# A transformer block with adaptive layer norm: three small moves around the K, Q and first MLP stages

## The chip, the cores and the metric

The kernel runs on one core of one Trainium2 chip. The metric is device time in microseconds (us); lower is better. The median of three runs of the kernel before is 244.02 us (243.87 to 244.14). One profiled execution of it took 243.82 us; its trace spans 242.1 us from the first to the last instruction, and all moments below are us from the start of that span.

## The reference

One block of a diffusion transformer: two batches of 256 tokens, width D = 1152, two heads of 576, MLP width F = 4608. A conditioning vector `c` gives six modulation vectors; the ones that matter here are `shift_a` and `scale_a` (first layer norm) and `shift_m` and `scale_m` (second).

```python
mod = (_silu(c) @ w_mod).reshape(B, 6, 1, D)
shift_a, scale_a, gate_a, shift_m, scale_m, gate_m = [mod[:, i] for i in range(6)]
h = _layernorm(x, axis=-1) * (1 + scale_a) + shift_a
qkv = (h @ wqkv).reshape(B, N, 3, H, Dh)
q, k, v = (qkv[:, :, 0].copy(), qkv[:, :, 1].copy(), qkv[:, :, 2].copy())
attn = _softmax(jnp.einsum('bqhd,bkhd->bhqk', q, k) * Dh ** (-0.5), axis=-1)
a = jnp.einsum('bhqk,bkhd->bqhd', attn, v).reshape(B, N, D) @ wo
x = x + gate_a * a
h2 = _layernorm(x, axis=-1) * (1 + scale_m) + shift_m
m = _gelu(h2 @ w_fc1) @ w_fc2
return x + gate_m * m
```

A shift added to all keys of a batch moves every score of one query by the same amount, which the softmax cancels. So the kernel computes K from `hT0` (normalized and scaled, not yet shifted) and adds `shift_a` only afterwards, for Q and V.

## The kernel before

P is 128, KD = D/P = 9 chunks of the width, T = 512 tokens. Activations are held transposed: chunk k is a tile of 128 features by 512 tokens, 256 of each batch b.

**Loads for K.** `w_k` has nine rows of 128 inputs. Columns 0 to 767 of each row come in a load of their own; the last 384 columns of all nine rows come in one load behind them, and then the shift weights. All loads of this part go through one queue (SyncE's).

```python
KGROUPS = [(0, 2), (2, 4), (4, 6), (6, 9)]
KM1 = 6
for g, (k0, k1) in enumerate(KGROUPS):
    load_scale_group(g, nc.sync)
    for k in range(k0, k1):
        nc.sync.dma_start(w_k[:, k, 0:KM1 * P], wqkv_v[:, k, D:D + KM1 * P])
nc.sync.dma_start(w_k[:, :, KM1 * P:D], wqkv_v[:, :, D + KM1 * P:2 * D])
...
w_shift_a = load_section("w_shift_a", S_SHIFT_A)     # three loads of three rows
w_q = wide_tile("w_q")
...
```

**End of K, the shift section, start of Q.** Output tiles 0 to 5 of K accumulate row by row as chunks arrive; tiles 6, 7 and 8 follow as whole panels of nine matmuls (L318 in the trace). The shift section is 36 narrow matmuls (L432) into `pn`, which VectorE transposes into `shift_a` (L438). VectorE (L454) and ScalarE (L456) then add the shift to each half chunk, and Q starts (L511). `k_evac(8)` copies K's last tile out of PSUM (L305 on VectorE); its accumulator is the one that Q's sixth matmul needs.

```python
k_panel(6)
k_evac(6)
k_panel(7)
k_evac(7)
k_panel(8, 0, 5)
shift_a = vec_section(sT, w_shift_a, "shift_a")
k_panel(8, 5)

hT = act.tile([P, KD, T], BF16, name="hT")
for k in range(KD):
    for b in range(B):
        dst, src = hT[:, k, b * N:(b + 1) * N], hT0[:, k, b * N:(b + 1) * N]
        if (k * B + b) % 3 < 2:
            nc.vector.tensor_scalar_add(dst, src, shift_a[:, k, b:b + 1])          # L454
        else:
            nc.scalar.activation(dst, src, ACT.Identity, bias=shift_a[:, k, b:b + 1])  # L456
    if k == 2:
        k_evac(8)
...
pq = [acc_tile([P, T], "pacc") for _ in range(KM1)]     # "acc" has 6 buffers
for k in range(KD):
    for m in range(KM1):
        nc.tensor.matmul(pq[m][:], w_q[:, k, m * P:(m + 1) * P], hT[:, k, :], ...)  # L511
```

**Second layer norm and the start of the MLP.** The output projection runs in groups (L705). Each is gated by VectorE (L710, reads PSUM), added to `x` by GpSimd (L711; VectorE for two of them) and measured by VectorE (L717). A normalized token tile t goes through a transposing DMA (L676) into `hT`; each chunk is then modulated in place: for batch 0 by ScalarE (L687) but for chunk 8, which is GpSimd's (L683); for batch 1 by ScalarE or VectorE (L691). The MLP's first matmul stage (FC1, L802) begins with batch 0 and takes chunks 0 to 8 in order.

```python
def ln2_modulate(b, ks=range(KD)):
    for k in ks:
        h = hT[:, k, b * N:(b + 1) * N]
        if b == 0 and k == KD - 1:
            nc.gpsimd.tensor_scalar(h, h, scale_m[:, k, b:b + 1], shift_m[:, k, b:b + 1], ...)   # L683
        elif b == 0 or k % 3 == 2:
            nc.scalar.activation(h, h, ACT.Identity, bias=shift_m[...], scale=scale_m[...])      # L687
        else:
            nc.vector.tensor_scalar(h, h, scale_m[...], shift_m[...], ...)                       # L691
...
wo_group(3, 0)
ln2_modulate(0, range(6))
ln2_stats(2, 2)
ln2_sqrt(2)
ln2_modulate(0, range(6, KD))
wo_group(3, 1)
ln2_stats(3, 0)
ln2_recip(2)
ln2_normalize(2)
ln2_transpose(2)
wo_group(3, 2)
wo_group(3, 3)
ln2_stats(3, 1)
ln2_stats(3, 2)
ln2_stats(3, 3)
ln2_sqrt(3)
ln2_recip(3)
ln2_normalize(3, 4 * P)
ln2_transpose(3)
...                                     # FC1, batch 0: 12 output tiles, then batch 1
```

[...]

Of the kernel before, what the change touches and what calls it, by code (L numbers as in the profile page):

```python
# [19 lines left out]
def kernel(  # L20
# [11 lines left out]
    nc = tc.nc  # L32
    B, N, D = x.shape
# [3 lines left out]
    P = 128  # L37
# [3 lines left out]
    KD = D // P  # L41
# [17 lines left out]
    def acc_tile(shape, name, dt=FP32):  # L59
        return psum.tile(shape, dt, name=name, tag="acc", bufs=6)  # L60
# [8 lines left out]
    wqkv_v = wqkv.rearrange("(k p) n -> p k n", p=P)  # L69
# [7 lines left out]
    def wide_tile(name):  # L77
        return wide.tile([P, KD, D], BF16, name=name, tag="wide")
# [19 lines left out]

    KGROUPS = [(0, 2), (2, 4), (4, 6), (6, 9)]
    KM1 = 6  # L100
    w_scale_a = wide_tile("w_scale_a")
    w_k = wide_tile("w_k")

    def load_scale_group(g, eng):
        c0, c1 = KGROUPS[g][0] * P, KGROUPS[g][1] * P
        eng.dma_start(w_scale_a[:, :, c0:c1], wmod_v[:, :, S_SCALE_A * D + c0:S_SCALE_A * D + c1])

    for g, (k0, k1) in enumerate(KGROUPS):
        load_scale_group(g, nc.sync)
        for k in range(k0, k1):  # L110
            nc.sync.dma_start(w_k[:, k, 0:KM1 * P], wqkv_v[:, k, D:D + KM1 * P])
    nc.sync.dma_start(w_k[:, :, KM1 * P:D], wqkv_v[:, :, D + KM1 * P:2 * D])

    def load_section(name, s, w=None):
        w = wide_tile(name) if w is None else w
# [12 lines left out]
    for r in range(0, KD, 3):  # L128
        nc.sync.dma_start(w_q[:, r:r + 3, 0:KM1 * P], wqkv_v[:, r:r + 3, 0:KM1 * P])
    nc.sync.dma_start(w_q[:, :, KM1 * P:D], wqkv_v[:, :, KM1 * P:D])  # L130
    w_scale_m = wide_tile("w_scale_m")
# [96 lines left out]
    def norm1(t, c0, c1, eng):  # L228
        if eng == "a":
            nc.scalar.activation(  # L230
                xns[t][:, c0:c1], x_sb[:, t, c0:c1], ACT.Identity,
                bias=nb1[:, t:t + 1], scale=rstd1[:, t:t + 1],
            )
        else:
            nc.vector.tensor_scalar(
                xns[t][:, c0:c1], x_sb[:, t, c0:c1], mv1[:, t, 0:1], rstd1[:, t:t + 1],
                op0=ALU.subtract, op1=ALU.mult,
            )
# [30 lines left out]
    def modulate(pt, i, k, t0, j0, w, eng):  # L269
        b = t0 // TPB  # L270
        dst, src, sc = hT0[:, k, t0 * P:t0 * P + w], pt[:, i, j0:j0 + w], scale_a[:, k, b:b + 1]
        if eng == "d":
            nc.vector.tensor_scalar_mul(dst, src, sc)
        else:
            nc.scalar.mul(dst, src, sc)
# [7 lines left out]

    def k_step(k, c0=0, c1=T, m0=0, m1=KM1):
        for m in range(m0, m1):
            if k == 0 and c0 == 0:
                pk[m] = acc_tile([P, T], "pk")
            nc.tensor.matmul(  # L288
                pk[m][:, c0:c1], w_k[:, k, m * P:(m + 1) * P], hT0[:, k, c0:c1],
                start=(k == 0 and c0 == 0), stop=(k == KD - 1), skip_group_check=True,  # L290
            )
# [19 lines left out]
    def k_evac(m):  # L311
        evac(kT[:, m, :], pk[m][:])

    def k_panel(m, ka=0, kb=KD):
        if ka == 0:
            pk[m] = acc_tile([P, T], "pk")
        for k in range(ka, kb):
            nc.tensor.matmul(  # L318
                pk[m][:], w_k[:, k, m * P:(m + 1) * P], hT0[:, k, :],
                start=(k == 0), stop=(k == KD - 1),  # L320
            )
# [70 lines left out]
    for k in range(2):  # L392
        modulate(pt_4, k, k, 3, 0, P, "d")
    k_step(3, 0, N, 3, KM1)
    norm1(1, CUT, D, "d")
# [31 lines left out]
    def vec_section(stat, w, name, nk=KD):  # L427
        pn = aux_tile([P, nk * 32], "pn")
        for k in range(KD):
            wk4 = w[:, k, :].rearrange("p (j q r) -> p q j r", q=4, r=32)  # L430
            for i in range(4):
                nc.tensor.matmul(  # L432
                    pn[32 * i:32 * i + SW, :].rearrange("p (j r) -> p j r", r=32),
                    stat[:, k, :], wk4[:, i, :, :],
                    start=(k == 0), stop=(k == KD - 1), tile_position=(0, 32 * i),
                )
        dst = act.tile([P, nk, 32], FP32, name=name)
        nc.vector.transpose(dst[:].rearrange("p k c -> p (k c)"), pn[:])  # L438
        return dst
# [2 lines left out]
    k_evac(6)  # L442
    k_panel(7)
    k_evac(7)
    k_panel(8, 0, 5)
    shift_a = vec_section(sT, w_shift_a, "shift_a")
    k_panel(8, 5)

    hT = act.tile([P, KD, T], BF16, name="hT")
    for k in range(KD):  # L450
        for b in range(B):
            dst, src = hT[:, k, b * N:(b + 1) * N], hT0[:, k, b * N:(b + 1) * N]
            if (k * B + b) % 3 < 2:
                nc.vector.tensor_scalar_add(dst, src, shift_a[:, k, b:b + 1])  # L454
            else:
                nc.scalar.activation(dst, src, ACT.Identity, bias=shift_a[:, k, b:b + 1])  # L456
        if k == 2:
            k_evac(8)
# [195 lines left out]
    def ln2_sqrt(t):  # L654
        nc.vector.bn_aggr(mv2[:, t, :], stats2[t][:, 0:nst[t], :].rearrange("p a b -> p (a b)"))
        rstds[t] = small.tile([P, 1], FP32, name="rstd", tag="rstd")
        nc.scalar.activation(rstds[t][:], mv2[:, t, 1:2], ACT.Sqrt, bias=eps_t[:], scale=1.0)

    def ln2_recip(t):
        nc.vector.reciprocal(rstds[t][:], rstds[t][:])  # L660
        nbs[t] = small.tile([P, 1], FP32, name="nb", tag="nb")
        nc.vector.tensor_scalar(nbs[t][:], mv2[:, t, 0:1], rstds[t][:], -1.0, op0=ALU.mult, op1=ALU.mult)

    def ln2_normalize(t, cs=D):
        xn2[t] = work.tile([P, D], BF16, name="xn", tag="xn", bufs=4)
        nc.scalar.activation(
            xn2[t][:, 0:cs], x1[:, t, 0:cs], ACT.Identity, bias=nbs[t][:], scale=rstds[t][:]
        )
        if cs < D:
            nc.vector.tensor_scalar(  # L670
                xn2[t][:, cs:D], x1[:, t, cs:D], mv2[:, t, 0:1], rstds[t][:],
                op0=ALU.subtract, op1=ALU.mult,
            )
# [5 lines left out]
# [4 lines that stand above are left out]
                nc.gpsimd.tensor_scalar(  # L683
                    h, h, scale_m[:, k, b:b + 1], shift_m[:, k, b:b + 1], op0=ALU.mult, op1=ALU.add,
                )
            elif b == 0 or k % 3 == 2:
                nc.scalar.activation(  # L687
                    h, h, ACT.Identity, bias=shift_m[:, k, b:b + 1], scale=scale_m[:, k, b:b + 1],
                )
            else:  # L690
                nc.vector.tensor_scalar(  # L691
                    h, h, scale_m[:, k, b:b + 1], shift_m[:, k, b:b + 1], op0=ALU.mult, op1=ALU.add,
                )
# [5 lines left out]
    def wo_group(t, i):  # L699
        b = t // TPB  # L700
        c0, c1 = cuts[t][i:i + 2]
        pacc = acc_tile([P, c1 - c0], "pacc")
        ks = [k for k in range(KD) if k != HC] + [HC]
        for k in ks:
            nc.tensor.matmul(  # L705
                pacc[:], aT[:, k, t * P:(t + 1) * P], w_o[:, k, c0:c1],
                start=(k == ks[0]), stop=(k == ks[-1]),
            )
        tmp = work.tile([P, c1 - c0], FP32, name="tmp", tag="tmp", bufs=3)
        nc.vector.tensor_tensor(tmp[:], pacc[:], gate_a[:, b, c0:c1], op=ALU.mult)  # L710
        (nc.vector if (t, i) in ((1, 2), (3, 3)) else nc.gpsimd).tensor_tensor(  # L711
            x1[:, t, c0:c1], tmp[:], x_sb[:, t, c0:c1], op=ALU.add
        )

    def ln2_stats(t, i):
        c0, c1 = cuts[t][i:i + 2]
        nc.vector.bn_stats(stats2[t][:, i, :], x1[:, t, c0:c1])  # L717
# [31 lines left out]
    ln2_stats(2, 1)  # L749
    wo_group(3, 0)  # L750
    ln2_modulate(0, range(6))
    ln2_stats(2, 2)
    ln2_sqrt(2)
    ln2_modulate(0, range(6, KD))
    wo_group(3, 1)
    ln2_stats(3, 0)
    ln2_recip(2)
    ln2_normalize(2)
    ln2_transpose(2)
# [49 lines left out]
    for b in range(B):  # L809
        for m0 in range(0, MSPLIT, 2):  # L810
            ms = range(m0, min(m0 + 2, MSPLIT))
            pacc = acc_tile([P, len(ms), N], "pacc")
            for m in ms:
                for k in range(KD):
                    f1_mm(pacc[:, m - m0, :], m, k, b * N, (b + 1) * N)
            if b == 0 and ms[-1] == MSPLIT - 3:
                ln2_modulate(1)
            nc.scalar.activation(gT[:, ms[0]:ms[-1] + 1, b * N:(b + 1) * N], pacc[:], ACT.Gelu_apprx_tanh)  # L818
# [41 lines left out]
    for gi, (n, t, c0, cw) in enumerate(groups):  # L860
        b = t // TPB
# [59 lines left out]
```

## Time and profile before

| what | value |
|---|---|
| median of 3 runs | 244.02 us (243.87 to 244.14) |
| span of the profiled execution | 242.1 us |
| TensorE (PE) busy | 235.3 us, 97% of the span |
| VectorE (DVE) busy | 93.4 us, 39% |
| ScalarE (ACT) busy | 69.5 us, 29% |
| GpSimd (POOL) busy | 32.0 us, 13% |
| granted TensorE clock | 1.000 |
| end of K, Q starts | 33.72 us |
| FC1 starts, and passes its first stop | 97.64 us, 98.75 us |
| FC2 starts | 168.35 us |

Read the table from the top: the time is the runs' median, and the trace tells where it goes. A row of the trace has the start of an instruction (or of a merged run of them), its length, the engine, the line of the kernel, and what is written from what. Matmuls are pipelined, so the distance from one start to the next, not the length of one, is what a matmul costs in a stream. A wait of TensorE shows as a distance between the end of one piece and the start of the next in the chain of work that ended last.

### The profile page before, as it was taken

Reading aid. Unit: us, or ns where it says so; the run is one execution under the profiler, and the core shown is the slowest. Engines: PE = TensorE matmul, PEld = TensorE weight load, DVE = VectorE, ACT = ScalarE, POOL = GpSimd, SP = SyncE. Lnnn points to the kernel's source line nnn. Section 1 sums busy time; section 2 is a strip of 40 time slices with the busy share of each in tenths; the row PEclk is TensorE's granted clock in tenths of the full one; section 3 lists DMA queues with packets and bytes.
Section 4 is the critical chain, followed back from the end, with each engine's and each line's share of the span. In section 5 each row is a group of like instructions: output and inputs, shape, how many; then the busy total and the mean of one; then the engine's idle time right before and its main releaser. Section 6 shows DMA issues by size and latency. Waiting matters only on the chain.

```text
span 242.1 us, 4031 instructions
## 1 busy us (share of the span) xinstructions
PE 235.3 (97%) x1698; PEld 142.7 (59%) x1698; DVE 93.4 (39%) x209; ACT 69.5 (29%) x138; POOL 32.0 (13%) x48
## 2 busy tenths in 40 slices
PE   8799999999999999999999999999999999999994
PEld 2486444466656666888844444444566656665573
DVE  2872550675694676720000019999002000000001
ACT  6532250543735174782222233322000000000000
POOL 1000400000310616300000000000314111111111
PEclk9999999999999999999999999999999999999999
DMA  6999999999999999799999999996891000000000
GB/s 223 324 330 360 379 344 247 326 372 284 254 322 361 380 255 208 208 219 327 327 328 249 191 274 328 327 326 188 245 286 39 19 16 16 20 20 27 19 19 16
DMA packets 76989, 54.48 MB, mean 225 GB/s; under 512 B 26011, under 2 KB 72491, under 8 KB 76971
## 3 DMA queue, kind: packets, MB, share of 16 engines
q1 hardware_dynamic: 76240, 53.02, 77.7%
q0 software_dynamic: 704, 1.20, 1.6%
q8 instruction: 13, 0.21, 0.4%
q14 instruction: 5, 0.04, 0.0%
q10 hardware_dynamic: 27, 0.00, 0.0%
HBM read 46.90 MB, written 1.19 MB: 199 GB/s over the span
## 4 chain that ended last, share of the span: by engine, by line
PE 91%; DMA 3%; ACT 2%; DVE 2%; issue 0%; SPq 0%; DVEq 0%
PE pacc L866 29%; PE pacc L802 29%; PE pacc L584 7%; PE pacc L705 6%; PE pacc L511 5%; PE pk L288 4%; DMA w_scale_a<-in_w_mod_dram 3%; PE pacc L519 2%; PE pk L318 2%; ACT hT L687 2%; PE pa L619 1%; PE ps_s L539 1%; PE pn L432 1%; PE pm L248 1%; PE pt L266 1%; PE pg L467 1%
## 5 line engine op out<-in xcount | busy, mean ns | idle before, releaser
L802 PE MATMUL pacc<-hT,w_f 128*128 128x256 bf16 (+1 forms) x432 | 70.5, 326 | 0.2 <-ACT hT L687 0.2
L866 PE MATMUL pacc<-w_f,gT 128*128 128x384 bf16 (+2 forms) x468 | 70.5, 314 | 0.0
L866 PEld LDWEIGHTS <-gT 128*128 128x128 bf16 x468 | 44.4, 98 | 26.2
L802 PEld LDWEIGHTS <-w_f 128*128 128x128 bf16 x432 | 42.2, 98 | 28.0 <-issue 0.4
L485 DVE SCALAR_TENSOR_TENSOR late<-w_gate_mT,late 128x1152 bf16<-128x1152 bf16 x18 | 24.4, 1358 | 36.8 <-DMA w_gate_mT<-in_w_mod_dram 36.2
L872 DVE TENSOR_TENSOR tmp<-pacc,gate 128x384 f32<-128x384 f32 (+2 forms) x13 | 6.8, 527 | 62.5 <-PE pacc L866 50.5
L840 ACT ACTIVATE gT<-pacc 128x512 bf16<-128x512 f32 x24 | 14.3, 597 | 32.3 <-PE pacc L802 32.3
L485 DVE SCALAR_TENSOR_TENSOR s_spill<-w_scale_m,s_b 128x1152 bf16<-128x1152 bf16 x12 | 16.3, 1357 | 8.5 <-DMA w_scale_m<-in_w_mod_dram 8.2
L705 PE MATMUL pacc<-w_o,big 128*128 128x384 bf16 (+2 forms) x117 | 17.9, 314 | 0.0
L874 POOL TENSOR_TENSOR o_sb<-tmp,x 128x384 bf16<-128x384 f32 (+1 forms) x12 | 11.7, 974 | 47.4 <-DVE tmp L872 47.4
L584 PE MATMUL pacc<-w_v,hT 128*128 128x384 bf16 x108 | 17.9, 326 | 0.0
L705 PEld LDWEIGHTS <-big 128*128 128x128 bf16 x117 | 11.0, 98 | 6.8 <-ACT big L627 0.2
L584 PEld LDWEIGHTS <-hT 128*128 128x128 bf16 x108 | 10.4, 98 | 7.0 <-issue 0.2
L288 PE MATMUL pk<-big,w_k 128*128 128x128 bf16 (+2 forms) x102 | 13.3, 278 | 0.0
L711 POOL TENSOR_TENSOR x<-tmp,x_sb 128x384 f32<-128x384 f32 (+1 forms) x11 | 9.8, 891 | 17.4 <-DVE tmp L710 9.5
L511 PE MATMUL pacc<-hT,w_q 128*128 128x512 bf16 x54 | 11.8, 379 | 0.1
L327 POOL DMA_DIRECT2D gates_dram<-grow x4 | 2.1, 521 | 70.8 <-DVE grow L826 70.8
L818 ACT ACTIVATE gT<-pacc 128x512 bf16<-128x512 f32 x12 | 6.9, 597 | 10.4 <-PE pacc L802 10.4
L288 PEld LDWEIGHTS <-w_k 128*128 128x128 bf16 x102 | 7.8, 98 | 3.0
L511 PEld LDWEIGHTS <-w_q 128*128 128x128 bf16 x54 | 5.3, 98 | 6.7 <-issue 0.4
L710 DVE TENSOR_TENSOR tmp<-pacc,gate 128x384 f32<-128x384 f32 (+2 forms) x13 | 6.7, 522 | 5.4 <-PE pacc L705 5.2
L523 ACT ACTIVATE big<-pacc 128x512 bf16<-128x512 f32 x9 | 4.8, 608 | 11.5 <-PE pacc L511 8.8
(101 smaller groups left out, 160.9 us busy)
## 6 DMA issues: line engine op xcount, KB each, us to landing
w_f<-in_w_fc_dram SPq DMA_DIRECT2D x14, 864.0 KB, 11.0
w_f<-in_w_fc_dram SPq DMA_DIRECT2D x2, 2592.0 KB, 10.7
w_f<-in_w_fc_dram SPq DMA_DIRECT2D x2, 1728.0 KB, 13.8
w_shift_a<-in_w_mod_dram SPq DMA_DIRECT2D x3, 864.0 KB, 10.5
w_v<-in_wqkv_dram SPq DMA_DIRECT2D x3, 864.0 KB, 6.0
w_gate_a<-in_w_mod_dram SPq DMA_DIRECT2D x3, 864.0 KB, 9.2
w_o<-in_wo_dram SPq DMA_DIRECT2D x3, 864.0 KB, 6.2
w_shift_m<-in_w_mod_dram SPq DMA_DIRECT2D x3, 864.0 KB, 13.0
```

Source lines behind the costliest of these rows:

```text
L288: nc.tensor.matmul(pk[m][:, c0:c1], w_k[:, k, m * P:(m + 1) * P], hT0[:, k, c0:c1], start=(k == 0 and c0 == 0), stop=(k == KD - 1), skip_g ...
L485: nc.vector.scalar_tensor_tensor(spill, wT[:, j, :], 1.0, s_b[b], op0=ALU.mult, op1=ALU.mult, accum_out=dst(j, b),)
L511: nc.tensor.matmul(pq[m][:], w_q[:, k, m * P:(m + 1) * P], hT[:, k, :], start=(k == 0), stop=(k == KD - 1),)
L584: nc.tensor.matmul(pacc[:], hT[:, k, t * P:(t + 1) * P], w_v[:, k, pnl * PW:(pnl + 1) * PW], start=(k == 0), stop=(k == KD - 1),)
L705: nc.tensor.matmul(pacc[:], aT[:, k, t * P:(t + 1) * P], w_o[:, k, c0:c1], start=(k == ks[0]), stop=(k == ks[-1]),)
L711: (nc.vector if (t, i) in ((1, 2), (3, 3)) else nc.gpsimd).tensor_tensor(x1[:, t, c0:c1], tmp[:], x_sb[:, t, c0:c1], op=ALU.add)
L802: nc.tensor.matmul(dst, w_f1[m // KD][:, k, ml * P:(ml + 1) * P], hT[:, k, c0:c1], start=(k == 0), stop=(k == KD - 1),)
L818: nc.scalar.activation(gT[:, ms[0]:ms[-1] + 1, b * N:(b + 1) * N], pacc[:], ACT.Gelu_apprx_tanh)
L840: nc.scalar.activation(gT[:, m, :], pacc[:], ACT.Gelu_apprx_tanh)
L866: nc.tensor.matmul(pacc[:], gT[:, kk, t * P:(t + 1) * P], w_f2[j][:, r, c0 - n * PW:c0 - n * PW + cw], start=(kk == 0), stop=(kk == KF - 1),)
L872: nc.vector.tensor_tensor(tmp[:], pacc[:], gate_m[:, b, c0:c0 + cw], op=ALU.mult)
L874: (nc.vector if last else nc.gpsimd).tensor_tensor(o_sb[:], tmp[:], x1[:, t, c0:c0 + cw], op=ALU.add)
```

## The change

Three moves. First, K's last panel is cut after 3 of its 9 matmuls instead of after 5, so that the shift section comes two matmuls earlier and six instead of four matmuls lie behind it. The division of the shift additions changes with it: VectorE takes all of batch 0 and the odd chunks of batch 1 (13 instead of 12), ScalarE the even chunks of batch 1 (5 instead of 6), so that the two halves of chunk 0 go to two engines. Second, rows 6 to 8 of `w_k` are loaded whole, and the load behind them shrinks to six rows. Third, chunks 6 and 7 of batch 0's second modulation go from ScalarE to VectorE, behind the statistics of the next tile; GpSimd's chunk 8 keeps its place.

```diff
     KM1 = 6
+    KWHOLE = 6
...
         for k in range(k0, k1):
-            nc.sync.dma_start(w_k[:, k, 0:KM1 * P], wqkv_v[:, k, D:D + KM1 * P])
-    nc.sync.dma_start(w_k[:, :, KM1 * P:D], wqkv_v[:, :, D + KM1 * P:2 * D])
+            c1 = KM1 * P if k < KWHOLE else D
+            nc.sync.dma_start(w_k[:, k, 0:c1], wqkv_v[:, k, D:D + c1])
+    nc.sync.dma_start(w_k[:, 0:KWHOLE, KM1 * P:D], wqkv_v[:, 0:KWHOLE, D + KM1 * P:2 * D])
...
-    k_panel(8, 0, 5)
+    k_panel(8, 0, 3)
     shift_a = vec_section(sT, w_shift_a, "shift_a")
-    k_panel(8, 5)
+    k_panel(8, 3)
...
-            if (k * B + b) % 3 < 2:
+            if b == 0 or k % 2:
                 nc.vector.tensor_scalar_add(dst, src, shift_a[:, k, b:b + 1])
             else:
                 nc.scalar.activation(dst, src, ACT.Identity, bias=shift_a[:, k, b:b + 1])
...
-            elif b == 0 or k % 3 == 2:
+            elif k < 6 if b == 0 else k % 3 == 2:
                 nc.scalar.activation(
...
     ln2_sqrt(2)
-    ln2_modulate(0, range(6, KD))
+    ln2_modulate(0, [KD - 1])
     wo_group(3, 1)
     ln2_stats(3, 0)
+    ln2_modulate(0, range(6, KD - 1))
     ln2_recip(2)
```

## Prediction, made before the changed kernel was run

> **What bounds the kernel now.** I read the page's first part, then the chain of work that ended last in order of time, then the timelines of the two spots the change touches, and last the DMA issues with their landings. The first part says TensorE is busy 97% of the span, so a change can only bring what it takes from TensorE's few stops. The chain shows where those are. Columns: start, length, what.
>
> ```profile
> 26.43 4.96 PE pk L318 x23
> 31.39 1.25 PE pn L432 x36
> 32.64 0.02 issue
> 32.66 0.49 DVE shift_a L438
> 33.16 0.02 issue
> 33.18 0.49 DVE hT L454 x2
> 33.67 0.04 issue
> 33.72 11.81 PE pacc L511 x54
> ...
> 97.53 0.19 ACT rstd L657
> 97.72 0.99 ACT hT L687 x2
> 98.71 0.04 issue
> 98.75 69.60 PE pacc L802 x425
> 168.35 70.30 PE pacc L866 x468
> ```
>
> The reader should see two places where the chain leaves TensorE: 32.64 to 33.72 (transpose the shift, add it to both halves of chunk 0, start Q), and up to 98.75 (ScalarE modulates chunks 6 and 7, FC1 goes on). From 98.75 to the end the two MLP stages stand almost without a break, so what is won before them should reach the end.
>
> In the first place TensorE is not idle all the time, for four matmuls of K's last panel lie there. Its own timeline:
>
> ```profile
> 32.54 1.04 PE L318 MATMUL pk<-big,w_k 128*128 128x512 bf16 x4
> 33.72 0.38 PE L511 MATMUL pacc<-hT,w_q 128*128 128x512 bf16 x1
> ```
>
> A matmul of 512 columns costs 0.216 us in a stream (23 in 4.96 us in the chain). Four started at 32.54 are streamed by 32.54 + 4 x 0.216 = 33.40. Q starts at 33.72. **Stop one: 0.32 us.**
>
> The second place, all engines:
>
> ```profile
> 97.00 0.92 POOL L711 TENSOR_TENSOR x<-tmp,x_sb 128x384 f32<-128x384 f32 x1
> 97.44 0.28 ACT L657 ACTIVATE rstd<-mv,eps_t 128x1 f32<-128x1 f32 x1
> 97.62 1.08 ACT L687 ACTIVATE hT<-hT,shift_m,scale_m 128x256 bf16<-128x256 bf16 x2
> 97.64 0.93 PE L802 MATMUL pacc<-hT,w_f 128*128 128x256 bf16 x7
> 98.58 0.67 POOL L711 TENSOR_TENSOR x<-tmp,x_sb 128x256 f32<-128x256 f32 x1 [0.66 <-DVE tmp L710]
> 98.73 0.66 DVE L711 TENSOR_TENSOR x<-tmp,x_sb 128x128 f32<-128x128 f32 x1
> 98.75 0.38 PE L802 MATMUL pacc<-hT,w_f 128*128 128x256 bf16 x2 [0.18 <-ACT hT L687]
> ```
>
> FC1's first seven matmuls (chunks 0 to 6) start at 97.64; at 256 columns one costs 0.109 us (half of 0.216, and 11 start in the 1.15 us after 98.75), so chunk 7's was due at 97.64 + 7 x 0.109 = 98.40. It starts at 98.75. **Stop two: 0.35 us.** The profile prints 0.18 as idle because a matmul's drawn length (0.27) is longer than its cost in the stream. Both stops together, 0.67 us, are the most that parts one and three can win.
>
> **What the Trainium skill says.** *TensorE: Matmul & The Clock Gate*, section "Back-to-back issue gap", gives 518 cycles at 2.4 GHz for 512 columns and 262 for 256: the trace agrees (0.216 and 0.109 us). *ScalarE: Activation LUTs*, section "What ACT_TABLE_LOAD costs", has 280 ns + 0.833 ns per element with one per-partition operand, about 93 ns more for a second, and an overlap of some 93 ns between neighbours: 493 and 586 ns for 256 elements; the trace has 492 for L456 and 586 for L687, a pace near 0.5 us. *VectorE: DVE Perf Modes*, "The perf-mode tier table", puts a bf16 tensor_scalar in SBUF in the fastest mode; the same job takes VectorE 346 ns (L691), six starting 106.3 to 107.6, a pace of 0.26 us. And *SBUF — State Buffer*, "SBUF: two separate sides", says that VectorE in a two-port mode (or with two SBUF inputs) and GpSimd share a port pair as an exclusive lock, held by whoever starts first for the whole instruction. The trace has one instance: VectorE's 128 x 128 addition at 98.73 lasts 0.66 us, though 384 columns took the same line 0.56 us at 86.57 with GpSimd quiet; GpSimd's addition runs from 98.58 to 99.25, and VectorE's ends at 99.39, 0.14 later. That bears on part three.
>
> **Part one, the split.** Nothing is removed; two matmuls move from before the shift section to behind it. The section, its transpose and the first additions come 2 x 0.216 = 0.43 us earlier: transpose from about 32.23, additions from 32.75. TensorE's work up to Q is unchanged, so its panel still ends at 33.40. When are both halves of chunk 0 ready? VectorE's half at 32.75 + 0.28 = 33.03; ScalarE's at 32.75 + 0.49 = 33.24, plus the 0.04 from engine to engine: 33.28. That is 0.12 before 33.40. Q starts at 33.40: **0.32 won.** VectorE's 13th addition costs 0.2 where it waits for transfers afterwards (8.2 us at L485), on no path.
>
> Next guard: Q's sixth matmul, due at 33.40 + 5 x 0.216 = 34.48, needs the accumulator of K's tile 8. VectorE is through its first four additions at about 32.75 + 0.87 = 33.62, the panel's last matmul is drawn to 33.58, and the copy takes 0.68: 34.3. Clear by 0.15 or so. Later chunks are needed only every 1.3 us, and VectorE and ScalarE make them faster.
>
> **Part two, the loads.** Three rows of 384 columns (96 KB each, 288 KB) go ahead of the last K load instead of in it. The queue moves about 0.34 MB per us in this stretch (windows from 14 to 22 us), so row 8 lands some 0.87 us later: issued at 14.6 with 6.2 to landing, 20.8 becomes 21.7. Its first use is the last of the 12 row matmuls that start at 23.84, so not before 25. No stop there. The shift weights behind it have the same bytes ahead, in fewer packets: their last load, issued at 19.3 with 11.4 to landing, is there at 30.7; the earlier section starts at 30.89 and reaches those rows at two thirds of its 1.25 us, 31.7. One us to spare. **Part two: 0.00.**
>
> **Part three, chunks 6 and 7.** ScalarE loses two modulations (0.99 us of chain); VectorE gets two, behind its statistics (L717) that start at 96.83 and give way at a pace of 0.48, so at 97.31. Alone, the first would end at 97.66, the second at 97.92, and chunk 7 is due at 98.40: the whole 0.35. But GpSimd's addition runs from 97.00 to 97.92. If the lock holds, VectorE's first modulation ends 0.14 to 0.35 after that (the two numbers: the tail seen at 99.39, or its whole length), 98.06 to 98.27, the second 0.26 on, 98.32 to 98.53; with 0.05 to TensorE chunk 7 goes at 98.40 to 98.58. The stop shrinks from 0.35 to between 0 and 0.18. I take **0.26 won**.
>
> What it costs elsewhere: the reciprocal for tile 2 (97.75 before) waits behind these two, up to 0.7 us, and so do tile 3's gating, statistics and transpose. Batch 1's modulation now starts at 106.3 and ends by 108.1; FC1 comes to batch 1 after 108 matmuls, near 109.7 (98.75 + 101 x 0.109). Its last chunk may be ready at 108.8 and is needed near 109.9, with everything moved by part one alike. It holds, with about 1 us.
>
> **Sum:** 0.32 + 0.00 + 0.26 = 0.58 us. 244.02 - 0.58 = **243.4 us**.
>
> **Rivals.** (a) *Only one stop goes.* The lock could cost more than I give it, or chunk 0's second half, now ScalarE's slower 0.49, could come after 33.40. For: the lock is visible once; ScalarE's margin is 0.12. Against: even at the late end chunk 7 beats ScalarE's 98.71. This gives 243.7. (b) *No lock for this instruction.* For: the one instance is an addition with two inputs, not a tensor_scalar. Both stops go whole: 243.35. (c) *The win is lost later.* TensorE comes 0.3 earlier to weights whose loads have not moved. Against: the profile has no TensorE wait for data after 21 us outside the two stops, and the loads have room (output projection: last landing near 74.5, first use 77.06; shift_m: 85.6 and 87.6). It gives 243.7 to 244.0. (d) *The delayed VectorE work stops FC1 at batch 1* or the larger K rows stop K: 244.0 to 244.5; margins of 1 us speak against it.
>
> **Range and chances.** The hard ceiling of 0.67 gives 243.35, and the spread of three runs before is 0.27, so I set the low end at 243.0. The high end covers (a) and (c): 243.8. The threshold of 2% is 4.9 us, far beyond what any step can move: faster by over 2% 0.01, within 2% 0.98, slower 0.01.
>
> **What would show it right or wrong.** Right: the shift section starts near 30.9, six K matmuls stand behind it, and Q's first matmul follows them without a gap, near 33.4; no TensorE wait at FC1's seventh and eighth matmul, or one under 0.2; L691 eight times, its first around the end of GpSimd's addition and drawn longer than 346 ns. Wrong: a TensorE wait for `w_shift_a` or `w_k`, a gap ahead of Q's sixth matmul, a new stop where FC1 takes up batch 1, or chunk 7 still later than 98.4 by the old amount.

## The result, and the profile after

The changed kernel takes 242.91 us (median of 6 runs, 242.34 to 243.20), the kernel before 243.84 us beside it (6 runs, 243.59 to 244.14). The ratio is 0.9959 with a 95% interval of 0.9945 to 0.9973: 0.66 to 1.34 us faster, where 0.58 was predicted. 242.91 lies 0.09 below the range.

The profiled execution of the changed kernel took 243.12 us, 0.70 less than that of before. Its chain of work, in order of time (start, length, what; the line numbers are two or three higher than before, so L320 is the old L318, L513 the old L511, L805 the old L802):

```profile
26.35 4.53 PE pk L320 x21
30.88 1.22 PE pn L434 x36
32.10 1.40 PE pk L320 x6
33.50 11.65 PE pacc L513 x54
...
88.53 8.90 PE pacc L707 x63
97.43 70.20 PE pacc L805 x432
167.63 70.30 PE pacc L869 x468
```

Both detours of the chain are gone: no transpose, addition or ScalarE modulation stands in it between 12 us and the end of the last matmul. This is the first stop in the timeline of all engines:

```profile
32.03 1.47 PE L320 MATMUL pk<-big,w_k 128*128 128x512 bf16 x6
32.15 0.48 DVE L440 STREAM_TRANSPOSE shift_a<-pn 128x288 f32<-128x288 f32 x1 [3.13 <-PE pn L434]
32.67 0.87 DVE L456 TENSOR_SCALAR hT<-big,shift_a 128x256 bf16<-128x256 bf16 x4
...
33.34 1.03 PE L513 MATMUL pacc<-hT,w_q 128*128 128x512 bf16 x4
33.54 0.69 DVE L307 CAST big<-pk 128x512 bf16<-128x512 f32 x1
```

Six matmuls at 0.216 us from 32.03 end at 33.33; Q starts at 33.34. And the second, with FC1's first matmul at 97.27:

```profile
96.46 0.55 DVE L719 BATCH_NORM_STATS2 stats<-x 128x6 f32<-128x384 f32 x1
96.63 0.92 POOL L713 TENSOR_TENSOR x<-tmp,x_sb 128x384 f32<-128x384 f32 x1
96.91 0.28 ACT L659 ACTIVATE rstd<-mv,eps_t 128x1 f32<-128x1 f32 x1
96.93 0.96 DVE L693 TENSOR_SCALAR hT<-hT,scale_m,shift_m 128x256 bf16<-128x256 bf16 x2
...
97.27 2.89 PE L805 MATMUL pacc<-hT,w_f 128*128 128x256 bf16 x25
97.81 0.15 DVE L662 RECIPROCAL rstd<-rstd 128x1 f32<-128x1 f32 x1
```

FC1 runs through from 97.27. VectorE's two modulations take 0.96 us together and are done at 97.89; chunk 7 is due at 97.27 + 7 x 0.109 = 98.03.

Q starts 0.38 us earlier than before (33.72 to 33.34; 0.07 of it is an earlier start of this execution), FC1 0.37 earlier (97.64 to 97.27), FC2 0.72 earlier (168.35 to 167.63). So in this pair of traces the first stop gave 0.31 and the second its whole 0.35. Together that is 0.66 of the 0.70 between these two executions (the earlier start makes up the rest), and less than the 0.93 of the medians. The experiments ask what the parts are worth one by one, and what the rest is.

### The profile page after: what moved, and what is told of

It is laid out like the page before. It is cut to its first block, busy times and chain, and to the rows that moved or that the text cites. A ratio compares the mean times of both kernels' runs of the same rounds, so it can differ in the third digit from the quotient of the medians.

```text
span 241.3 us, 4034 instructions
## 1 busy us (share of the span) xinstructions
PE 235.0 (97%) x1698; PEld 142.8 (59%) x1698; DVE 94.4 (39%) x212; ACT 68.2 (28%) x135; POOL 32.0 (13%) x48
## 4 chain that ended last, share of the span: by engine, by line
PE 94%; DMA 3%; DVE 1%; ACT 0%; SPq 0%; issue 0%; DVEq 0%
PE pacc L869 29%; PE pacc L805 29%; PE pacc L707 7%; PE pacc L586 7%; PE pacc L513 5%; PE pk L290 4%; DMA w_scale_a<-in_w_mod_dram 3%; PE pk L320 2%; PE pacc L521 2%; PE pa L621 1%; PE ps_s L541 1%; PE pn L434 1%; PE pm L250 1%; PE pt L268 1%; PE pg L469 1%; SPq L85 0%
## 5 line engine op out<-in xcount | busy, mean ns | idle before, releaser
L805 PE MATMUL pacc<-hT,w_f 128*128 128x256 bf16 (+1 forms) x432 | 70.4, 326 | 0.0
L805 PEld LDWEIGHTS <-w_f 128*128 128x128 bf16 x432 | 42.2, 98 | 27.7
L707 PE MATMUL pacc<-w_o,big 128*128 128x384 bf16 (+2 forms) x117 | 17.9, 314 | 0.0
L586 PE MATMUL pacc<-w_v,hT 128*128 128x384 bf16 x108 | 17.9, 326 | 0.0
L513 PE MATMUL pacc<-hT,w_q 128*128 128x512 bf16 x54 | 11.8, 379 | 0.0
L513 PEld LDWEIGHTS <-w_q 128*128 128x128 bf16 x54 | 5.3, 98 | 6.4
```

Of the source, the lines that this page charges most:

```text
L586: nc.tensor.matmul(pacc[:], hT[:, k, t * P:(t + 1) * P], w_v[:, k, pnl * PW:(pnl + 1) * PW], start=(k == 0), stop=(k == KD - 1),)
L707: nc.tensor.matmul(pacc[:], aT[:, k, t * P:(t + 1) * P], w_o[:, k, c0:c1], start=(k == ks[0]), stop=(k == ks[-1]),)
L805: nc.tensor.matmul(dst, w_f1[m // KD][:, k, ml * P:(ml + 1) * P], hT[:, k, c0:c1], start=(k == 0), stop=(k == KD - 1),)
```

## The experiments

**A measure of the second stop.** From FC1's first matmul to FC2's first takes 70.36 us in the changed kernel (97.27 to 167.63), where TensorE has no stop. In any other trace, this distance minus 70.36 is the stop. The table below uses it. From Q's first matmul to FC1's took 63.92 or 63.93 us in thirteen of the fourteen traces and 64.08 in that of part one alone, so what is won at Q does reach FC1.

**The whole change once more** (no edit).

> The whole change once more. Theory A: 0.66 to 0.7 us faster, the sum of the three parts, so that the 0.93 of the first comparison was partly chance. Theory B and C: 0.9 us again.

Measured: 243.01 us against 243.52, ratio 0.9977 (0.9968 to 0.9987), 0.32 to 0.78 us faster. FC1 to FC2 is 70.36 again, Q follows six K matmuls without a gap. With the first comparison only 0.66 to 0.78 fits both; a single comparison of this size is not sharper than that.

**Part one alone: the split and the new division.**

```diff
-    k_panel(8, 0, 5)
+    k_panel(8, 0, 3)
     shift_a = vec_section(sT, w_shift_a, "shift_a")
-    k_panel(8, 5)
+    k_panel(8, 3)
...
-            if (k * B + b) % 3 < 2:
+            if b == 0 or k % 2:
```

> Only the split of K's last panel at 3 and the new division of the shift additions. Theory A (the gain is the two stops, each removed whole, 0.31 and 0.35 us, and the rest of the measured 0.93 is the varying start of the runs): 0.31 us faster, Q's first matmul without a gap behind six K matmuls, stop two still there at FC1's eighth matmul. Theory B (the whole loads of K bring the missing 0.2 to 0.3 us): 0.31 here as well. Theory C (each stop is worth more than its gap in the trace, because all that follows shifts against the loads): 0.4 to 0.5 us.

Measured: 243.61 us, ratio 1.0000 (0.9984 to 1.0015). All three theories wanted at least 0.31 us. The medians show no gain, though the interval, from 0.37 us slower to 0.39 faster, still holds 0.31. In the trace Q's gap is gone (K's panel ends and Q starts at 33.13). This execution took 244.46 us, 0.85 above the median of its kernel, and its chain shows where the win went:

```profile
89.52 0.93 ACT xn L666
90.44 0.02 issue
90.46 4.55 DMA hT<-xn
95.01 0.02 issue
95.03 0.04 ACTq L687
95.07 0.05 issue
95.12 3.06 ACT hT L687 x6
98.17 0.18 ACT rstd L657
98.36 0.99 ACT hT L687 x2
99.35 0.04 issue
99.39 0.71 PE pacc L802 x5
```

ScalarE normalized tile 1 and the transposing DMA went out at 90.46, 0.4 earlier than before (90.9). But it landed at 95.01, later than before's 94.4, and ScalarE's eight modulations hang on that landing. For the kernel before, the profile names something else as what ScalarE waited for:

```profile
93.91 0.55 DVE L717 BATCH_NORM_STATS2 stats<-x 128x6 f32<-128x384 f32 x1
...
94.48 3.06 ACT L687 ACTIVATE hT<-hT,shift_m,scale_m 128x256 bf16<-128x256 bf16 x6 [3.60 <-DVE stats L717]
```

The statistics ended at 94.46 and the DMA landed at 94.4, so this trace alone can't tell the two apart. Where the chain runs through the landing, the modulation starts 0.10 to 0.11 us after it (here 95.01 to 95.12), and 94.4 and 94.48 fit that. The runs that move only loads, below, decide it. TensorE, 0.43 earlier at FC1 (97.21), stopped three times:

```profile
97.21 0.80 PE L802 MATMUL pacc<-hT,w_f 128*128 128x256 bf16 x5
98.22 0.27 PE L802 MATMUL pacc<-hT,w_f 128*128 128x256 bf16 x1 [0.22 <-ACT hT L687]
98.90 0.27 PE L802 MATMUL pacc<-hT,w_f 128*128 128x256 bf16 x1 [0.41 <-ACT hT L687]
99.39 0.38 PE L802 MATMUL pacc<-hT,w_f 128*128 128x256 bf16 x2 [0.22 <-ACT hT L687]
```

The stop is 1.42 us here instead of 0.35. In this execution, TensorE's win at Q was paid back at FC1, and more.

**Part two alone: the whole K rows.**

```diff
+    KWHOLE = 6
...
-            nc.sync.dma_start(w_k[:, k, 0:KM1 * P], ...)
-    nc.sync.dma_start(w_k[:, :, KM1 * P:D], ...)
+            c1 = KM1 * P if k < KWHOLE else D
+            nc.sync.dma_start(w_k[:, k, 0:c1], ...)
+    nc.sync.dma_start(w_k[:, 0:KWHOLE, KM1 * P:D], ...)
```

> Only K's last three rows loaded whole. Theory A: 0.00, within 0.1 us of the kernel before, both stops in their old size. Theory B: 0.2 to 0.3 us faster, with an earlier end of K or earlier landings that TensorE had waited for.

Measured: 243.55 us, ratio 0.9998 (0.9986 to 1.0010). No gain shows, as predicted. Its trace has one more size of the second stop: 0.65 us, with ScalarE's first modulation at 94.93.

**Part three alone: chunks 6 and 7 on VectorE.**

```diff
-            elif b == 0 or k % 3 == 2:
+            elif k < 6 if b == 0 else k % 3 == 2:
...
-    ln2_modulate(0, range(6, KD))
+    ln2_modulate(0, [KD - 1])
     wo_group(3, 1)
     ln2_stats(3, 0)
+    ln2_modulate(0, range(6, KD - 1))
```

> Only chunks 6 and 7 of batch 0 on VectorE. Theory A: 0.35 us faster, no TensorE wait in FC1's first nine matmuls; the first of the two modulations still drawn near 0.7 us because GpSimd's addition runs into it, the second near 0.34. My prediction's lock as sized there: 0.26, with a rest of the stop of 0.1.

Measured: 243.20 us, ratio 0.9985 (0.9976 to 0.9994), 0.15 to 0.58 us faster. FC1 to FC2 takes 70.36: the stop is gone whole.

**The question now** was whether the stop belongs to a landing that does not move with TensorE. The transposing DMAs share SyncE's queue with FC1's weights, and two loads of 864 KB each are issued ahead of them. So I moved one load behind them, in three settings, and in a fourth moved another load ahead.

**Part one alone, with the later load.** Chunks 6 and 7 stay on ScalarE.

```diff
     load_f1(0, 0)
-    load_f1(0, 1)
...
     ln2_transpose(1)
+    load_f1(0, 1)
     load_f1(0, 2)
```

> Part one alone, and the second load of FC1's first weight tile is issued behind the two transposing DMAs of batch 0 instead of ahead of them; chunks 6 and 7 stay on ScalarE. Theory L (FC1's first stop is set by the landing of the second transposing DMA, which lies behind that load in the queue and does not come forward with TensorE, so part one alone is paid back there): the landing comes 1 us or more earlier (before 94.4, part one alone 95.0), the stop at FC1's eighth matmul goes, and part one's 0.31 shows up with the 0.35 of the stop: 0.6 to 0.8 us faster than the kernel before, without part three. Rival (part one is worth nothing for some other reason, as a loss in attention or a chance of these runs): the landing comes earlier or not, and the time stays within 0.2 us of part one alone.

Measured: 243.19 us against 243.70, ratio 0.9974 (0.9965 to 0.9984), 0.39 to 0.85 us faster, where part one alone showed no gain. The edit touches no computation. How much of this is part one's win, and how much the later load's own, is a question for the later load alone, below. ScalarE's timeline (the lines are one lower here than before):

```profile
89.52 0.92 ACT L665 ACTIVATE xn<-x,nb,rstd 128x640 bf16<-128x640 f32 x1 [0.53 <-issue]
93.84 3.06 ACT L686 ACTIVATE hT<-hT,shift_m,scale_m 128x256 bf16<-128x256 bf16 x6 [3.40 <-DMA hT<-xn]
```

The normalization starts at the same 89.52 as in part one alone, and the modulations 1.28 us earlier (95.12 to 93.84). The landing takes 3.3 us from its issue instead of 4.6. Against the kernel before it came only 0.6 earlier, not the 1 us I expected, and a stop of 0.14 is left.

**The whole change, with the later load** (same edit).

> The whole change with the same later load. Theory L: TensorE already has no stop here in most executions, so 0.0 to 0.2 us faster than the whole change, 0.6 to 0.8 us faster than the kernel before; landing 1 us or more earlier. Rival (the load is the next thing FC1 waits for): a new TensorE wait on its weights near FC1's 28th matmul, slower than the whole change.

Measured: 242.99 us, ratio 0.9967 (0.9955 to 0.9979), 0.51 to 1.09 us faster. FC1 to FC2 70.37. No wait for the later weights. Its interval overlaps that of the whole change, so it can't be called better; its 9 runs lie between 242.69 and 243.25.

**Parts one and three, without the whole K rows.**

> Parts one and three without the whole loads of K. Theory A and L: as the whole change, 0.5 to 0.7 us faster than the kernel before. Theory B (the loads matter once the section is earlier): 0.2 us or more slower than the whole change, with a TensorE wait for the shift weights.

Measured: 242.99 us, ratio 0.9966 (0.9956 to 0.9976), 0.58 to 1.07 us faster: as good as the whole change. Here ScalarE's modulations began late, at 94.61, and FC1 still ran through in 70.36.

**The later load alone,** on the kernel before.

> The kernel before with nothing but the later issue of FC1's second weight load. Theory L: the second transposing DMA lands 3.3 us after its issue, about 94.2, as it did in the two kernels with this load behind it; ScalarE's eight modulations then end 0.2 earlier and stop two shrinks from 0.35 or more to about 0.15: 0.2 to 0.4 us faster. Rival (the landing follows from something else): no change beyond 0.1.

Measured: 243.37 us against 243.88, ratio 0.9977 (0.9965 to 0.9988), 0.29 to 0.85 us faster; FC1 to FC2 70.48, so a stop of 0.12. The stop came out as expected, the gain above the middle of it. Even its low end of 0.29 is more than the 0.23 by which the stop shrank between the two traces, so on average the stop of the kernel before must be larger than the 0.35 of its one trace, if the gain is all the stop's. The runs fit a stop that varies: the 11 with the later load lie within 0.51 us (243.16 to 243.67), the 33 of the kernel before within 1.28 (243.38 to 244.66). And the gain is about as large as that with part one added (0.39 to 0.85), so these runs do not show that part one's win comes back with the later load.

**One more load ahead,** on the kernel before.

```diff
     load_f1(0, 1)
+    load_f1(0, 2)
...
     ln2_transpose(1)
-    load_f1(0, 2)
```

> The opposite of the later load, on the kernel before: FC1's third weight load (864 KB) is also issued ahead of the two transposing DMAs. Theory L: at some 0.34 MB per us the queue is held 2.6 us longer, so the second transpose lands up to that much later, near 97 instead of 94.4. The stop follows the rule found so far: start of ScalarE's first modulation minus start of FC1's first matmul, plus 3.51 us, so near 3 us, and the kernel is 2 to 2.7 us slower. Rival (the landing does not hang on the loads ahead): no change beyond 0.3 us.

Measured: 245.00 us against 243.51, ratio 1.0069 (1.0051 to 1.0088), 1.24 to 2.14 us slower. From its chain:

```profile
91.37 4.13 DMA hT<-xn
...
95.61 3.06 ACT hT L688 x6
98.86 0.99 ACT hT L688 x2
99.89 23.19 PE pacc L802 x210
```

The landing is at 95.50, 1.1 us later than before, not 2.6: the size of the load is no measure of the delay, the direction is right. The last load ahead of the transposes landed at 93.2 (81.8 + 11.4) instead of 91.0 (74.9 + 16.1). About 0.5 of the 1.1 us is a later issue of the second transpose (91.37 instead of 90.90). The stop is 71.91 - 70.36 = 1.55.

All traces in which ScalarE does eight modulations, together (the last two rows are runs that follow below). a is the start of ScalarE's first modulation, s that of FC1's first matmul; eight modulations with a square root in front of the last two take 4.27 us to TensorE (94.48 to 98.75 before), and chunk 7 is due 0.76 after s, so the rule is stop = a - s + 3.51. It fits the kernel before by construction; the other rows test it.

| kernel | s | a | stop by the rule | stop by FC1's length |
|---|---|---|---|---|
| before | 97.64 | 94.48 | 0.35 | 0.35 |
| part one | 97.21 | 95.12 | 1.42 | 1.42 |
| part two | 97.80 | 94.93 | 0.64 | 0.65 |
| part one, later load | 97.21 | 93.84 | 0.14 | 0.14 |
| later load alone | 97.31 | 93.92 | 0.12 | 0.12 |
| one more load ahead | 97.58 | 95.61 | 1.54 | 1.55 |
| the split alone | 96.96 | 93.88 | 0.43 | 0.43 |
| the new division alone | 97.79 | 94.43 | 0.15 | 0.15 |

**The split without the new division.**

> Only the split at 3; the shift additions divided as before, both halves of chunk 0 on VectorE. By the arithmetic of the first stop the second half is ready at 0.49 us after the transpose's end, 0.15 ahead of the end of the panel: Q's first matmul follows the six K matmuls without a gap, as with the new division. Theory L on the time: paid back at FC1's first stop, 0.0 to 0.15 us faster than the kernel before. Rival (the new division is what opens Q): a gap of 0.05 to 0.3 us ahead of Q.

Measured: 243.80 us against 243.88, ratio 0.9997 (0.9985 to 1.0008). Q follows six K matmuls without a gap with both halves on VectorE: six from 31.73 end at 33.03, and Q starts at 33.03. The new division is not what opens Q. In time no gain shows again (from 0.20 us slower to 0.37 faster), though in this trace the stop at FC1 grew only to 0.43.

**The new division without the split.**

> Only the new division of the shift additions, split at 5 as before. ScalarE's half of chunk 0 takes 0.49 where VectorE's two took 0.49 together, so Q starts at the same moment: the gap ahead of Q stays at 0.28 to 0.32. Rival (the division opens Q): the gap shrinks by 0.2 or more.

One execution, 243.79 us. Its timeline, TensorE and ScalarE:

```profile
32.66 1.04 PE L318 MATMUL pk<-big,w_k 128*128 128x512 bf16 x4
...
33.30 0.91 ACT L456 ACTIVATE hT<-big,shift_a 128x256 bf16<-128x256 bf16 x2 [2.24 <-DVE shift_a L438]
...
33.86 0.38 PE L511 MATMUL pacc<-hT,w_q 128*128 128x512 bf16 x1 [0.16 <-ACT hT L456]
```

Four matmuls end at 33.52 and Q starts at 33.86: a gap of 0.34, as large as before. The stop at FC1 is 0.15 here, with the loads as before. One slow half on ScalarE takes as long as two fast ones on VectorE.

**GpSimd's addition moved to VectorE,** to see whether it is what stretches the first modulation.

```diff
-        (nc.vector if (t, i) in ((1, 2), (3, 3)) else nc.gpsimd).tensor_tensor(
+        (nc.vector if (t, i) in ((1, 2), (3, 1), (3, 3)) else nc.gpsimd).tensor_tensor(
```

> The whole change, but GpSimd's addition of the group in question (tile 3, second group) goes to VectorE, ahead of the two modulations there. Lock theory: with GpSimd quiet the first modulation is drawn at 0.34 us like the others, not 0.70, and the second starts 0.26 behind it. Rival (the 0.70 comes from something else, a semaphore or the statistics in front of it): it stays near 0.7. Both modulations end later by the addition moved in front, about 0.5 us, so a small stop of TensorE may return.

One execution, 243.15 us. In the changed kernel, the eight modulations on VectorE have these durations (line of one source, in ns: min, median, max):

```profile
L693 DVE TENSOR_SCALAR hT<-hT,scale_m,shift_m x8: 335/340/702, 96.9 to 107.2; 128x256 bf16<-128x256 bf16 x8
```

and with GpSimd quiet:

```profile
L693 DVE TENSOR_SCALAR hT<-hT,scale_m,shift_m x8: 330/341/346, 97.4 to 107.2; 128x256 bf16<-128x256 bf16 x8
...
97.42 0.59 DVE L693 TENSOR_SCALAR hT<-hT,scale_m,shift_m 128x256 bf16<-128x256 bf16 x2
```

The 702 ns are gone. The two end at 98.01, with chunk 7 due at 97.17 + 0.76 = 97.93, and a stop of 0.13 returns, as expected.

## Why the prediction was wrong

**Bound, and the first stop: right.** The working said "Q starts at 33.40: 0.32 won". The six matmuls, the transpose 0.43 earlier and the free gap all stand in the trace; the first stop gave 0.31. Beside the trace's 0.216 us for a matmul the prediction sets 518 cycles from *TensorE: Matmul & The Clock Gate*, "Back-to-back issue gap"; that section gives them for an isolated matmul and about 131 ns for 512 columns in a stream, and here the stream itself shows 0.216 us (54 matmuls of Q in 11.65 us). ScalarE's margin of 0.12 held, and so did the accumulator of K's tile 8. My reason for the division was loose: the split alone opens Q.

**Part two: right.** Predicted 0.00; alone it measures a ratio of 0.9998 (0.9986 to 1.0010), and without it the other two parts do as well as the whole. The shift weights' last load landed at 17.9 + 13.0 = 30.9 in the changed kernel; its rows are used near 31.6.

**Part three: the mechanism right, a size off.** The lock between GpSimd and VectorE, from *SBUF — State Buffer*, "SBUF: two separate sides", is shown: the first modulation is drawn at 702 ns beside GpSimd's addition and at 346 or less without it. But it cost TensorE nothing. I let it end 0.14 to 0.35 after GpSimd; it ended 0.08 after (96.93 + 0.70 = 97.63, GpSimd at 97.55), and chunk 7 was ready 0.14 before it was due. So "0.26 won" should have read the whole stop, and this is 0.09 of the difference.

**The step that failed: "Stop two: 0.35 us"** as a fixed size, and on it "Both stops together, 0.67 us, are the most that parts one and three can win" and "The hard ceiling of 0.67", from which the low end of the range was set. The size was exact for the one execution I read. But the stop is the distance between two clocks: TensorE, which brings s, and the transposing DMA, which brings a. The traces of kernels in which ScalarE modulates eight chunks, with the loads as before, show 0.35, 0.65, 1.42, 0.43 and 0.15. What part three does is take two of eight modulations off that path, so that the last ScalarE chunk is needed no earlier than a can bring it, and FC1 runs through even with a at 94.61, where the rule for eight gives 0.81.

I had the loss of part one's win as rival (c), "TensorE comes 0.3 earlier to weights whose loads have not moved", and looked only at the margins of weights. One of these was misread: the last load of the output projection landed at 78.4 (67.6 + 10.8), not near 74.5, though no stop of TensorE came of it. The transposes' landing was in the same table of transfers (3.2 to 6.1 us from issue to landing for four like transfers), and that spread should have widened the low end.

**How much of the miss this is.** From 244.02 - 0.58 = 243.44 to 242.91 are 0.53 us. Of these 0.18 are the kernel before itself, 243.84 in the comparison and 244.02 in the three runs I started from; their spread of 0.27 was too small a measure of chance, for 59 later runs of the same kernel spread over 1.58 us (243.10 to 244.68). Another 0.09 is the lock's tail. The other 0.26 would need a second stop of 0.61 on average. That is not shown: the second comparison gave 0.51 between the medians, a little less than predicted, so the first, with 0.93, may owe this part to chance.

**What is shown and what is not.** That loads ahead of the transposes set the stop is shown by moving nothing but loads: one less ahead made the kernel before 0.29 to 0.85 us faster, one more 1.24 to 2.14 slower, and the landing and the stop moved the same way. Whether they share the queue or only the DMA engines behind it, no run separates. That part one's win is lost at this stop on average is not shown. One trace has it lost (a stop of 1.42), in the trace of the split alone the stop grew by only 0.08, and the intervals of both kernels still hold 0.31. Nor is it shown that the two parts add up to less apart than together: the medians of 0.09 slower and 0.32 faster stand against 0.51 for the whole in the same comparison, and the intervals overlap. What makes the queue run later in one execution than in another stays open. So does the exact gain: the two comparisons of the same kernel gave 0.66 to 1.34 and 0.32 to 0.78 us, and my 0.58 lies in the second and not in the first.

## What to carry to other kernels

A stop that ends with a DMA's landing has no fixed size: read it as the difference of two clocks, look at the spread of the landing, and don't call its size in one trace a ceiling. A win on the engine that bounds the kernel can be lost where the next thing it meets does not move forward too, as in the trace of part one alone, so look for the next landing behind it before adding up gains. Where a short, urgent transfer shares a queue with large loads that are not due for a while, issue those behind it.

## What the runs showed of the hardware

The second of two transposing DMAs of 128 x 1152 bf16 from SBUF to SBUF took 3.3 us from issue to landing in the three kernels with one of FC1's weight loads of 864 KB ahead of it, and 3.3 to 4.6 us in the ten with two; the first of the two took between 4.2 and 7.2 us. A third load of 864 KB ahead delayed the second landing by 1.1 us, much less than the 2.6 us that its bytes take at the 0.34 MB per us of the prediction. And a VectorE modulation that started while GpSimd's addition ran was drawn as one long instruction (702 instead of about 340 ns), not as idle time in front of it; it ended 0.08 us after the addition.
